# Chunked attention and a token mixer on one core: a table of steps in place of a planner, with other homes and another order for loads and stores

## The chip, the core and the metric

The kernel runs on one core of one Trainium2 chip. The core has TensorE (PE in the profile, with PEld for its weight loads), VectorE (DVE), ScalarE (ACT), GpSimd (POOL), SyncE (SP) and 16 DMA engines, with SBUF as working memory and PSUM, in eight banks, for what TensorE writes. The metric is the device time of one execution in microseconds (us): the median of three runs before the change is 141.73, with 141.18 and 142.25 as the ends. The profile is of one further execution, of 140.38 us, whose span from first to last instruction is 138.6.

## The reference

Inputs q, k and v have 8 batches, 8 heads, 576 tokens and 64 channels, all 32-bit floats. Attention is inside chunks of 64 tokens; its output, heads side by side (512 channels), goes through a mixer over tokens.

```python
scores = scale * np.matmul(q_c, k_c.transpose(0, 1, 2, 4, 3))   # chunks of 64 tokens
scores = scores - np.max(scores, axis=-1, keepdims=True)
attn = np.exp(scores)
attn = attn / (np.sum(attn, axis=-1, keepdims=True) + 1e-09)
out = np.matmul(attn, v_c)
...
x = out.transpose(0, 2, 1, 3).reshape(B, S, H * D)
wq = x @ w_q
wk = x @ w_k
W_tok = scale * np.einsum('bsd,btd->bst', wq, wk)
mixed = np.einsum('bst,btd->bsd', W_tok, x)
return (np.maximum(mixed, 0.0) @ w_out).astype(np.float32)
```

The kernel multiplies in another order: mixed = wq (wk^T x), with wk^T x a matrix of 64 by 512 for a batch, called G.

## The kernel before, in words

**Units.** Work is cut into 20 "pairs". A whole pair is 256 tokens of a batch (2 x 128); a batch has two of them and 64 tokens left over, and the left-over tokens of two batches make a small pair. For each two batches the order is whole, whole, small, whole, whole: pairs 0 to 4 are batches 0 and 1, with pair 2 small, and so on up to pair 19. Pairs 2, 7, 12 and 17 are small.

**Steps of a pair.** PE transposes q and k (`tq`, L476, L461 for a small pair), ACT or DVE copy the results to SBUF (`qbd`, `kt`), PE makes scores (`S`, L496), DVE takes the maximum and subtracts it (L509, L520), ACT takes the exponential (L530), PE transposes that (`E`, L542), it is copied (`et`), PE multiplies with v (`V`, L572, two halves of a whole pair; a column of ones beside v gives the sum), DVE divides (L584, L588, L598, tile `xs`). Then come the transposes of xs (`xT`, L614), the projection (`pj`, L624, copied to `wt`), and the transposed weights (`wkT`, L641). Per batch PE makes G (L680, copied to `g`); per pair it then makes the mixed tokens (`mix`, L721), ACT or DVE take the positive part (`rm`, L739 and L741), PE multiplies with w_out (`out`, L755) and ACT or DVE copy the result to the tile `osb`, from which SP stores it (L769 to L775). All copies are at L401.

**Shapes of the array.** Most matmuls use the whole 128 x 128 array. L476 and L680 write 64 columns ("tall" in the code), L572 works in quarters of 64 x 64 ("quart").

**Order.** A planner, `plan` (L51), runs while the program is built. It has costs and due times for each step (`RANK`, `ENGINE`), plays the engines through and emits each step on the engine and PSUM bank that it picked; on every engine the steps then stand in that fixed order. Where PE would be idle in the first 26 us of that plan it puts matmuls on a tile of ones (`idle`, L788).

**Loads.** GpSimd issues them, pair by pair: q and k, then v of the same pair; the mixer's weights come behind pair 1 (`wqk`) and pair 3 (`wo`). They convert to 16 bits on the way. Pair 0's q and k come through SP in 32 bits, into two homes of `osb`. q and k of whole pairs have 11 homes in turn (`NQK`), v of all pairs has one place each in `v_all`, `osb` has four homes (`NOSB`). Eight counters serve GpSimd's loads in turn, so a load is issued when the one eight before it has landed.

**Stores.** SP issues them in program order: the first half of a whole pair (128 tokens, 256 KB) as soon as it is copied, the second half as two stores of 128 KB since its two blocks of 64 tokens lie swapped in the tile; for a small pair two of 128 KB.

Of the kernel before, what the change touches and what calls it, by code (L numbers as in the profile page):

```python
# [17 lines left out]
class Node:  # L18


    def __init__(self, kind, prio, cost, emit, deps, forms=(), takes=(), reads=None, size=0):
        self.kind, self.prio, self.cost, self.emit = kind, prio, cost, emit
        self.deps, self.forms, self.takes, self.reads = deps, forms, list(takes), reads
        self.size = 2 * size
        self.frees = None
        self.form = self.eng = self.done = None
        if reads is not None:
            reads.readers += 1


class Banks:


    def __init__(self, n):
        self.n, self.readers, self.left, self.at, self.end = n, 0, 0, None, 0.0
        self.by = None


TAIL = {"PE": 0.17, "DVE": 0.09, "ACT": 0.1}
BEGIN = {"PE": 1.5, "DVE": 4.9, "ACT": 3.4}  # L40
SWITCH = {
    ("full", "tall"): 0.1,
    ("tall", "full"): 0.21,
    ("full", "quart"): 0.155,
    ("quart", "full"): 0.15,
    ("quart", "tall"): 0.11,
    ("tall", "quart"): 0.17,
}


def plan(nodes, look, idle, sem=0.05, banks=8):  # L51

    free_at = [0.0] * banks
    held = [False] * banks
    users, waiting = {}, {}
    for n in nodes:  # L60
        waiting[n] = sum(d.done is None for d in n.deps)
        for d in n.deps:
            users.setdefault(d, []).append(n)
    clock = dict(BEGIN)
    ready = [n for n in nodes if n.cost and not waiting[n]]
    loads = [n for n in nodes if n.kind == "load"]
    form, order = None, []
    count, fetched = 0, [0.0, 0.0, 3.0]

    def place(n, at):  # L70
        taken, spots = set(), []
        for bk in n.takes:
            best = None
            for i in range(0, banks, bk.n):
                span = range(i, i + bk.n)
                if any(held[x] or x in taken for x in span):
                    continue
                t = max(free_at[x] for x in span) + sem
                buddy = i ^ 1
                lone = bk.n == 1 and not held[buddy] and free_at[buddy] + sem <= at  # L80
                key = (max(t, at), lone, -t, i)
                if best is None or key < best[0]:
                    best = (key, i)
            if best is None:
                return None, None
            taken.update(range(best[1], best[1] + bk.n))
            spots.append(best[1])
            at = max(at, best[0][0])
        return at, spots

    while ready:
        options = {}
        for n in ready:
            there = max([d.done + sem for d in n.deps], default=0.0)
            pick = None
            for e, cost in n.cost.items():
                at = max(clock[e], there)
                if n.reads is not None and n.reads.by not in (None, e):
                    at = max(at, n.reads.end + 0.03)
                if e == "PE":  # L100
                    if form is not None and form not in n.forms:
                        at = max(at, clock[e] + SWITCH[form, n.forms[0]])
                    at = max(at, fetched[(count + n.size) // 256] - cost / 2)
                    cost *= 2 if at < COLD else 1
                if pick is None or at + cost < pick[0]:
                    pick = (at + cost, at, e)
            _, at, e = pick
            at, spots = place(n, at)
            if at is not None:
                options.setdefault(e, []).append((at, n.prio, len(order), n, spots))  # L110
        best = None
        for e, found in options.items():
            soonest = min(o[0] for o in found)
            stay = [e == "PE" and form in o[3].forms for o in found]
            some = [
                (o[1] - BONUS * same, o[0], o)
                for o, same in zip(found, stay)
                if o[0] <= soonest + (max(look, STAY) if same else look)
            ]
            o = min(some, key=lambda s: s[:2])[2]  # L120
            if best is None or o[0] < best[0]:
                best = (o[0], e, o[3], o[4])
        at, e, n, spots = best
        while e == "PE" and clock[e] < WARM:
            cols = 512 if at - clock[e] > 0.4 and clock[e] > COLD else 256
            cost = cols / (1200 if clock[e] < COLD else 2360)
            spot = next((i for i in reversed(range(banks)) if not held[i] and free_at[i] + sem < clock[e]), None)
            if spot is None or at - clock[e] <= 0.15:
                break
            emit = lambda f, spot=spot, cols=cols: idle(spot, cols)  # L130
            w = Node("idle", 0.0, {"PE": cost}, emit, [], forms=("full",), size=1)
            w.eng, w.form, form, w.start = e, "full", "full", clock[e]
            clock[e] += cost
            w.done = free_at[spot] = clock[e] + TAIL[e]
            if (count + w.size) // 256 > count // 256:
                fetched.append(w.start + FETCH[0])
            count += w.size
            order.append(w)
        for bk, i in zip(n.takes, spots):
            bk.at, bk.left = i, bk.readers  # L140
            for x in range(i, i + bk.n):
                held[x] = True
        if e == "PE":
            if form not in n.forms:
                form = n.forms[0]
            n.form = form
            if (count + n.size) // 256 > count // 256:
                fetched.append(at + n.cost[e] / 2 + (FETCH[0] if at < FETCH[2] else FETCH[1]))
            count += n.size
        n.eng, n.start = e, at  # L150
        clock[e] = at + n.cost[e] * (2 if e == "PE" and at < COLD else 1)
        n.done = clock[e] + TAIL[e]
        if n.reads is not None:
            bk = n.reads
            bk.left -= 1
            bk.end, bk.by = max(bk.end, n.done), e
            if not bk.left:
                for x in range(bk.at, bk.at + bk.n):
                    held[x], free_at[x] = False, bk.end
        if n.kind == "osb":  # L160
            for x in loads:
                if x.done > n.done:
                    x.done += STORE
        if n.frees is not None:

            late = max(n.done + HOME - x.done for x in loads if x.first == n.frees)
            for x in loads:
                if x.first >= n.frees and late > 0:
                    x.done += late
        ready.remove(n)  # L170
        for u in users.get(n, ()):
            waiting[u] -= 1
            if not waiting[u]:
                ready.append(u)
        order.append(n)
    return order


LAG = {"tq": -0.31, "S": -3.7, "E": 1.53, "V": -7.38, "x": -6.59, "xT": 2.38, "pj": -2.9, "G": -8.16, "mix": 3.34, "out": 4.56}
LOOK = 0.107  # L180
CLEAR, STAY, BONUS = 0.0, 0.0, 0.0
COLD, WARM = 5.0, 26.0
NQB, NG, NQK, NOSB = 3, 3, 11, 4
STORE, HOME = 0.7, 5.5
FETCH = (6.4, 3.7, 100.0)


RANK = [
# [62 lines left out]
def kernel(  # L251
# [31 lines left out]
    for b in range(0, B, 2):  # L283
        for bb, ms in ((b, range(NPB)), (b, [None]), (b + 1, range(NPB))):
            for m in ms:
                pairs.append((bb, m))
                first.append(NU)
                NU += 1 if m is None else 2
# [99 lines left out]
    def vec(n):  # L388
        return n / 960 + 0.066
# [434 lines left out]
```

## Time and profile before

| | |
|---|---|
| median of three runs | 141.73 us |
| profiled execution | 140.38 us |
| its span | 138.6 us |
| PE, DVE, ACT, POOL busy | 127.3, 114.0, 98.5, 74.0 us |
| matmuls on ones (L788) | 73, 16.2 us busy |
| loads (software queue) | 14.29 MB written to SBUF in 78736 packets |
| store and first-load queue | 10.49 MB in 7584 packets |
| HBM read, written | 29.62 MB, 9.44 MB |

The profile's slices cut the span into 40 parts and give the busy tenths of each engine in each part. A line of the timeline has the start, the time it took, the engine, the line of the code, the operation, and in brackets how long the engine was idle before it and what ended that. PE's matmuls overlap each other in such rows, so the step between starts tells more than the time taken. A load's or a store's landing is when its completion is counted.

### The profile page before, as it was taken

To read this page: it belongs to the slowest core of one execution; us is meant where nothing else is said; L and a number is where in the kernel's file an instruction comes from. 1 tells how busy PE (TensorE), PEld (TensorE's weight loads), DVE (VectorE), ACT (ScalarE), POOL (GpSimd) and SP (SyncE) were. 2 spreads that over 40 slices of the span, in tenths; PEclk is the share of its full clock that TensorE was granted. 3 is DMA by queue.
4 is the path that set the end of the run, shared out by engine and by line. 5 is a ranking of instruction groups with operands and counts; after the bars stand their busy time and mean duration, and the time that the engine had idled before them with its cause. 6 is when DMAs were issued, how large, how long until landed. Compare 5 with 4: busy or idle time off the path is not lost.

```text
span 138.6 us, 5196 instructions
## 1 busy us (share of the span) xinstructions
PE 127.3 (92%) x2205; PEld 89.5 (65%) x2205; DVE 114.0 (82%) x223; ACT 98.5 (71%) x177; POOL 74.0 (53%) x95
## 2 busy tenths in 40 slices
PE   6999999989997999989999999899997999899950
PEld 4566577667676676777767786687676666665410
DVE  4777969579999999999999999989989798871510
ACT  3255584668883998878968968977596497895730
POOL 7997998576499677344898555629900000000000
PEclk9999999999999999999999999999999999999998
DMA  3999999999999999999999999999999943315484
GB/s 92 271 176 155 140 162 179 172 178 169 165 263 203 202 173 215 238 224 200 155 204 220 238 173 206 212 200 188 190 225 264 127 137 90 123 34 137 168 236 142
DMA packets 86343, 25.11 MB, mean 181 GB/s; under 512 B 79152, under 2 KB 81712, under 8 KB 86320
## 3 DMA queue, kind: packets, MB, share of 16 engines
q0 software_dynamic: 78736, 14.29, 127.4%
q1 hardware_dynamic: 7584, 10.49, 24.4%
q8 instruction: 17, 0.28, 0.7%
q14 instruction: 6, 0.05, 0.1%
HBM read 29.62 MB, written 9.44 MB: 282 GB/s over the span
## 4 chain that ended last, share of the span: by engine, by line
PE 59%; DVE 26%; ACT 8%; issue 4%; DVEq 0%
PE ps L755 15%; PE ps L476 10%; PE ps L788 6%; PE ps L721 5%; DVE mx L509 5%; PE ps L496 5%; PE ps L614 4%; DVE xs L598 4%; PE ps L542 4%; DVE sh L520 4%; PE ps L624 4%; PE ps L572 3%; ACT es L530 2%; DVE xt L401 2%; DVE qbd L401 2%
## 5 line engine op out<-in xcount | busy, mean ns | idle before, releaser
L755 PE MATMUL ps<-wo,rm 128*128 128x512 f16 x144 | 36.0, 379 | 0.0
L356 POOL DMA_DIRECT2D v_all<-in_v_dram x32 | 28.9, 919 | 2.5 <-DMA wo<-in_moe_w_out_dram 1.5
L509 DVE TENSOR_REDUCE mx<-ps 128x16 f32<-128x1024 f32 (+1 forms) x20 | 22.3, 1114 | 4.4 <-PE ps L496 2.0
L598 DVE TENSOR_TENSOR xs<-ps,rec 128x512 f16<-128x512 f32 x36 | 24.0, 687 | 0.4
L401 ACT COPY osb<-ps 128x512 f32<-128x512 f32 x30 | 17.5, 587 | 5.9 <-PE ps L755 5.6
L530 ACT ACTIVATE es<-sh 128x1024 f16<-128x1024 f32 (+1 forms) x20 | 19.5, 974 | 2.3 <-DVE sh L520 1.8
L476 PE MATMUL ps<-ident,qk 128*64 128x128 f16 x512 | 20.6, 222 | 0.3
L476 PEld LDWEIGHTS <-qk 128*64 128x64 f16 x512 | 16.0, 109 | 6.7 <-issue 4.3
L520 DVE TENSOR_TENSOR sh<-ps,mx 128x1024 f32<-128x1024 f32 x16 | 19.5, 1219 | 0.3
L755 PEld LDWEIGHTS <-rm 128*128 128x128 f16 x144 | 12.5, 98 | 11.0 <-ACT rm L741 0.4
L401 ACT COPY qbd<-ps 64x512 f32<-64x512 f32 (+1 forms) x29 | 15.5, 536 | 4.1 <-PE ps L476 3.6
L741 ACT ACTIVATE rm<-ps 128x1024 f16<-128x1024 f32 (+1 forms) x14 | 16.1, 1164 | 2.4 <-PE ps L721 2.2
L788 PE MATMUL ps<-ones 128*128 128x256 f16 (+1 forms) x73 | 16.2, 346 | 1.5 <-DVE ones L300 1.2
L344 POOL DMA_DIRECT2D qk<-in_k_dram x15 | 13.5, 902 | 4.8 <-DMA qk<-in_k_dram 4.2
L344 POOL DMA_DIRECT2D qk<-in_q_dram x15 | 13.6, 906 | 4.5 <-DMA qk<-in_q_dram 2.6
L496 PEld LDWEIGHTS <-qbd 128*128 128x128 f16 x288 | 10.6, 98 | 3.5 <-issue 1.3
L496 PE MATMUL ps<-kt,qbd 128*128 128x64 f16 x288 | 11.7, 193 | 0.7 <-DVE xs L598 0.4
L542 PE MATMUL ps<-ident,es 128*128 128x128 f16 x144 | 11.3, 220 | 0.5 <-ACT es L530 0.4
L614 PE MATMUL ps<-ident,xs 128*128 128x128 f16 x144 | 11.2, 219 | 0.2 <-DVE xs L598 0.2
L721 PE MATMUL ps<-wt,g 128*128 128x256 f16 (+1 forms) x96 | 10.8, 246 | 0.5 <-DVE g L401 0.3
L624 PE MATMUL ps<-xt,wqk 128*128 128x256 f16 (+1 forms) x80 | 10.9, 262 | 0.0
L572 PE MATMUL ps<-v_all,et 64*64 64x65 f16 x576 | 9.6, 195 | 1.4 <-issue 1.1
(56 smaller groups left out, 181.7 us busy)
## 6 DMA issues: line engine op xcount, KB each, us to landing
out_dram<-osb SPq DMA_DIRECT2D x40, 128.0 KB, 5.2
v_all<-in_v_dram POOLq DMA_DIRECT2D x32, 128.0 KB, 9.0
out_dram<-osb SPq DMA_DIRECT2D x16, 256.0 KB, 5.7
qk<-in_q_dram POOLq DMA_DIRECT2D x15, 256.0 KB, 8.8
qk<-in_k_dram POOLq DMA_DIRECT2D x15, 256.0 KB, 9.4
osb<-in_q_dram SPq DMA_DIRECT2D x1, 512.0 KB, 4.0
osb<-in_k_dram SPq DMA_DIRECT2D x1, 512.0 KB, 5.0
qk<-in_q_dram POOLq DMA_DIRECT2D x8, 64.0 KB, 8.3
```

Source lines behind the costliest of these rows:

```text
L344: nc.gpsimd.dma_start(qk[u][:, t], rows)
L356: nc.gpsimd.dma_start(v_all[:, first[u] + i, :, 0:D], rows)
L401: (nc.vector.tensor_copy if eng == "DVE" else nc.scalar.copy)(to, of)
L476: nc.tensor.transpose(tp[half(o), j, :, r, :], of, ident[:])
L496: nc.tensor.matmul(sp[:, i, j, c, :], lhsT=st["qb", u][:, j, x].rearrange("p o s -> p (o s)"), rhs=st["kt", u][:, j, x * C : x * C + C], s ...
L509: nc.vector.tensor_reduce(mx[:], scores(), axis=AX.X, op=ALU.max)
L520: nc.vector.tensor_tensor(out=sh[:].rearrange("p x (g r) -> p x r g", r=R), in0=in_banks(bs, 512).rearrange("p i (x r g) -> p (i x) r g", ...
L530: nc.scalar.activation(es[:].rearrange("p x s -> p (x s)"), st["sh", u][:].rearrange("p x s -> p (x s)"), AF.Exp, scale=scale_attn,)
L598: nc.vector.tensor_tensor(out=to, in0=xp()[:, :, :, 0:D], in1=by, op=ALU.mult)
L721: nc.tensor.matmul(ma[:, o, f, s], lhsT=st["g", bb][:, c0 : c0 + P], rhs=st["wt", u][:, s], start=True, stop=True,)
L755: nc.tensor.matmul(op[c, :], lhsT=st["rm", u][:, f, i * P + c.start : i * P + c.stop], rhs=wo[:, f, :], start=(f == 0), stop=(f == NF - 1),)
L788: nc.tensor.matmul(ps[:, i, 0:cols], lhsT=ones[:, 0:P], rhs=ones[:, 0:cols], start=True, stop=True)
```

## The change

The planner and its tables go; the program has one table, `ORDER`, with a step, its engine (p, a, v) and its PSUM bank in each word, and `i` for a matmul on ones with its bank and its columns. The table has 63 of those where the planner put 73. `HOMES` gives each tile its number of homes: q and k of whole pairs 7, `osb` 13, `wt` and `wk` 8 where they had 6. v of whole pairs goes into a ring of 8 homes of two slots each (`NV`); small pairs keep their own. `LOADS` gives the order of loads: q and k of the next pair stand ahead of v of this one. A load of v into a used home is emitted right behind the product with v of the pair that had it (`load_more`).

Before the first store SP gets a small read of `v_all`, into a tile `held`. A whole pair is stored in two stores of 256 KB (64 partitions, two blocks each) once both halves are copied. The second half of the last pair is made and stored in two parts of 256 columns, and its v is loaded turned, in two loads, so that its tokens lie in order.

```diff
+NQB, NG, NV = 3, 3, 8
...
+HOMES = {
+    "qk": 7,
+    "osb": 13,
...
+LOADS = "q1 v0 q2 v1 wqk v2 q3 v3 wo q4 q5 v4 q6 v5 q7 v6 q8 v7 q9 v8 q10 v9 q11 v10 q12 v11 q13 v12 q14 v13 q15 v14 q16 v15 q17 v16 q18 v17 q19 v18 v19"
+ORDER = """
+1a 0v 3v 2a i7.256 i6.256 i5.256 i7.256 i6.256 i5.256 i7.256 i6.256 i5.256 i7.256 i6.256 i5.256 i7.256 i6.256
...
+448a 309a 503a 524p1 449p0 422p7 397p6 525v 483v 423a 450v 504p4 424p7 558p0 555p5 526v 484v 398v 505a 425a
...
+615v 551p5 608p2 609v 623a 624p4 616p6 620p7 552a 625a 610p4 618p5 612p2 617v 621v 613v 611a 619a
+"""
-    v_all = const.tile([P, NU, H, VW], F16, name="v_all")
+    v_all = const.tile([P, 2 * NV + B // 2, H, VW], F16, name="v_all")
...
+    heir_v = dict(zip(whole, whole[NV:]))
+    slot = {u: 2 * (n % NV) for n, u in enumerate(whole)}
+    slot.update({u: 2 * NV + n for n, u in enumerate(rests)})
...
+    made_v = {None: 2}
+
+    def load_more():
+        while loads and made_v.get(loads[0][2], 0) == 2:
+            load, args, _ = loads.pop(0)
+            load(*args)
+
+    load_more()
...
+            def pe_v(fours=fours, xp=xp):
...
+                made_v[u] = made_v.get(u, 0) + 1
+                load_more()
...
+            wide = DM // 2 if (b, m, i) == (B - 1, NPB - 1, 1) else DM
+            for at in range(0, DM, wide):
...
+                def ev_o(eng, i=i, bo=bo, s=s, wide=wide):
+                    if not osb:
+                        osb.append(home("osb", [P, 2, DM], F32))
+                    copy(eng, osb[0][:, i, s], in_banks(bo, wide)[:, 0])
+                    if not held:
+
+                        held.append(const.tile([1, 2], F16, name="held"))
+                        last = slot[len(pairs) - 1]
+                        nc.sync.dma_start(held[0][:], v_all[P - 1 : P, last + 1, H - 1, D - 2 : D])
+                    done.append(s)
+                    if m is None:
+                        for c in range(2):
+                            nc.sync.dma_start(out[b + c, S - C : S, :], osb[0][half(c), i, :])
+                    elif turned(u, 1):
+                        t0 = 2 * P * m + i * P
+                        nc.sync.dma_start(out[b, t0 : t0 + P, s], osb[0][:, i, s])
+                    elif len(done) == 2:
+                        rows = out[b, 2 * P * m : 2 * P * m + 2 * P, :].rearrange("(x p) d -> p x d", p=C)
+                        for c in range(2):
+                            nc.sync.dma_start(rows[:, 1:3] if c else rows[:, 0:4:3], osb[0][half(c)])
...
+    steps = [n for n in nodes if n.cost]
+    for e in ORDER.split():
+        what, eng, *at = re.split(r"([ipav])", e, maxsplit=1)
+        at = [int(x) for part in at for x in part.split(".") if x]
+        if eng == "i":
+            nc.tensor.matmul(ps[:, at[0], 0 : at[1]], lhsT=ones[:, 0:P], rhs=ones[:, 0 : at[1]], start=True, stop=True)
+            continue
+        n = steps[int(what)]
+        for bk, i in zip(n.takes, at):
+            bk.at = i
+        n.emit(*{"p": (), "a": ("ACT",), "v": ("DVE",)}[eng])
```

More of the change, by code (lines that the diff above doesn't have):

```diff
@@ L1 @@
 import math
+import re
 from contextlib import ExitStack
@@ L18, with __init__ @@
 class Node:
[L21 to L26, printed above, removed]
+    def __init__(self, kind, cost, emit, deps, form=None, takes=(), reads=None, size=0):
+        self.kind, self.cost, self.emit, self.deps = kind, cost, emit, deps
+        self.form, self.takes, self.reads, self.size = form, list(takes), reads, 2 * size
+        self.frees = self.pair = self.done = None
         if reads is not None:
@@ L34, in __init__ @@
     def __init__(self, n):
[L35 to L47, printed above, removed]
-}
[L51 to L176, printed above, removed]
@@ L273 @@
     VW = D + 2
-    QUART, TALL, FULL = ("quart",), ("tall",), ("full",)
+    QUART, TALL, FULL = "quart", "tall", "full"
     const = ctx.enter_context(tc.tile_pool(name="const", bufs=1))
-    work = ctx.enter_context(tc.tile_pool(name="work", bufs=3))
+    work = ctx.enter_context(tc.tile_pool(name="work", bufs=1))
     psum = ctx.enter_context(tc.tile_pool(name="psum", bufs=1, space=PS))
     ctx.enter_context(tc.manual_schedule())
-    pairs, first, NU = [], [], 0
+    pairs = []
     for b in range(0, B, 2):
@@ L312, in half, with turned, home @@
         return slice(C * i, C * i + C)
+    def turned(u, i):
+        return u == len(pairs) - 1 and i == 1
+    def home(tag, shape, dtype=F16):
+        return work.tile(shape, dtype, name=tag, tag=tag, bufs=HOMES[tag])
     arrive, clk, wide_in = {}, 4.6, []
+    whole = [u for u, (b, m) in enumerate(pairs) if m is not None]
+    heir = dict(zip(whole[1:], whole[1 + HOMES["qk"] :]))
+    heir_v = dict(zip(whole, whole[NV:]))
+    rests = [u for u, (b, m) in enumerate(pairs) if m is None]
+    slot = {u: 2 * (n % NV) for n, u in enumerate(whole)}
+    slot.update({u: 2 * NV + n for n, u in enumerate(rests)})
     def landing(key, us):
@@ L357, in load_v @@
-        landing(("v", u), halves if m is None else 2 * halves)
-    whole = [u for u, (b, m) in enumerate(pairs) if m is not None and u]
-    heir = dict(zip(whole, whole[NQK:]))
-    for u in range(len(pairs)):
-        load_qk(u)
-        if u == 0:
-            make_identity(nc, ident[:])
-        load_v(u)
-        if u == 1:
-            for i, x in enumerate((moe_w_q, moe_w_k)):
-                nc.gpsimd.dma_start(wqk[:, :, i, :], x.rearrange("(f p) j -> p f j", p=P))
+        if m is None:
+            for i in range(2):
+                rows = v[b + i, :, S - C : S, :].rearrange("h p d -> p h d")
+                nc.gpsimd.dma_start(v_all[half(i), slot[u], :, 0:D], rows)
+            return
@@ new lines, in load_v, with load_w @@
+        for i in range(2):
+            t0 = 2 * P * m + i * P
+            for c in range(2) if turned(u, i) else [None]:
+                on, of = (slice(0, P), slice(t0, t0 + P)) if c is None else (half(1 - c), slice(t0 + c * C, t0 + c * C + C))
+                nc.gpsimd.dma_start(v_all[on, slot[u] + i, :, 0:D], v[b, :, of, :].rearrange("h p d -> p h d"))
+    def load_w():
+        for i, x in enumerate((moe_w_q, moe_w_k)):
+            nc.gpsimd.dma_start(wqk[:, :, i, :], x.rearrange("(f p) j -> p f j", p=P))
@@ L369, with load_wo @@
+    def load_wo():
+        nc.gpsimd.dma_start(wo[:], moe_w_out.rearrange("(f p) n -> p f n", p=P))
+    load_qk(0)
+    make_identity(nc, ident[:])
+    arrive["f32", 0], arrive["f32", 1] = 4.85, 6.2
+    loads = []
+    for e in LOADS.split():
+        u = int(e[1:]) if e[1:].isdigit() else None
+        rest = u is not None and pairs[u][1] is None
+        if e == "wqk":
             landing("w", 0.9)
-        if u == 3:
-            nc.gpsimd.dma_start(wo[:], moe_w_out.rearrange("(f p) n -> p f n", p=P))
+            loads.append((load_w, [], None))
+        elif e == "wo":
@@ L372 @@
             landing("wo", 3.3)
+            loads.append((load_wo, [], None))
+        elif e[0] == "q":
+            for t in range(2):
+                landing(("qk", u, t), 0.94 if rest else wide)
+            loads.append((load_qk, [u], None))
+        else:
+            landing(("v", u), halves if rest else 2 * halves)
+            loads.append((load_v, [u], next((w for w in heir_v if heir_v[w] == u), None)))
+    made_v = {None: 2}
[3 more added lines that the diff above has]
+            load(*args)
@@ L415 @@
             cost = {"ACT": act(512, True), "DVE": 0.4}
-            ready.setdefault(("cast", t), []).append(add("cast", -9.0, cost, ev, [landed(("f32", t))]))
+            ready.setdefault(("cast", t), []).append(add("cast", cost, ev, [landed(("f32", t))]))
     parts = [(("qb", n + 2), t[:], 0.95) for n, t in enumerate(qbd[2:])]
@@ L461, in pe @@
                         nc.tensor.transpose(tp[:, t, j, :], qk[u][:, t, 2 * j : 2 * j + 2, :], ident[:])
-            n1 = add("tq", pri, {"PE": 8 * 0.056}, pe, [landed(("qk", u, 1))], forms=FULL, takes=[bk], size=8)
+            n1 = add("tq", {"PE": 8 * 0.056}, pe, [landed(("qk", u, 1))], form=FULL, takes=[bk], size=8)
             for t in range(2):
@@ L476, in pe @@
                             nc.tensor.transpose(tp[half(o), j, :, r, :], of, ident[:])
-            n1 = add("tq", pri, {"PE": 8 * 0.056}, pe, ready["cast", t] if u == 0 else [landed(("qk", u, t))], forms=TALL, takes=[bk], size=16)
+            n1 = add("tq", {"PE": 8 * 0.056}, pe, ready["cast", t] if u == 0 else [landed(("qk", u, t))], form=TALL, takes=[bk], size=16)
             if u in heir:
```

263 lines of the change are left out of this document (127 added, 136 removed), and 39 rows, old and new, of the table RANK.

## The prediction

> **What bounds the kernel now.** I read the page first (shares, slices), then the stretches, the timeline of TensorE, and the landing of each load against its first use.
>
> In the page's slices PE, DVE and the DMA are all near full, at different ends:
>
> ```profile
> PE   6999999989997999989999999899997999899950
> ...
> DVE  4777969579999999999999999989989798871510
> ...
> DMA  3999999999999999999999999999999943315484
> GB/s 92 271 176 155 140 162 179 172 178 169 165 263 203 202 173 215 238 224 200 155 204 220 238 173 206 212 200 188 190 225 264 127 137 90 123 34 137 168 236 142
> ...
> L788 PE MATMUL ps<-ones 128*128 128x256 f16 (+1 forms) x73 | 16.2, 346 | 1.5 <-DVE ones L300 1.2 <-DVE ones L304 0.3
> ```
>
> Until 26.6 us PE is kept busy with L788, matmuls on ones that fill the wait for loads. After that there are none, and the DMA stays full until 110 us. Two stretches (columns: PE, PEld, DVE, ACT, POOL, granted clock, DMA share, GB/s):
>
> ```profile
> 32.60:133.60 101.00, 96.99 (x1711) 68.68 (x1709) 89.70 (x173) 80.29 (x145) 46.60 (x57) 1.00 1.50 186
> ...
> 30.00:100.00 70.00, 67.51 (x1280) 49.63 (x1277) 67.76 (x128) 56.70 (x101) 48.13 (x60) 1.00 1.88 201
> ```
>
> PE and DVE are both at 96 to 97% from 30 to 100 us, so a gain needs relief on both. The PE timeline shows where busy PE is not working:
>
> ```profile
> 64.25 1.03 PE L755 MATMUL ps<-wo,rm 128*128 128x512 f16 x4
> 65.21 0.64 PE L476 MATMUL ps<-ident,qk 128*64 128x128 f16 x16
> 65.77 0.32 PE L572 MATMUL ps<-v_all,et 64*64 64x65 f16 x16
> 66.03 0.81 PE L476 MATMUL ps<-ident,qk 128*64 128x128 f16 x16
> ```
>
> Four L755 take 0.865 when another such group follows, but 0.96 here, where the array's shape changes from 128x128 to 128x64. I added up, from starts in such rows, what each step takes back to back (transposes of q or k 0.57, scores 0.47, transposed weights 0.45, half of the product with v 0.19, xT 0.45, projection 0.44, G 0.55, mix 0.44, out 0.865; less for the small pairs). All steps come to 105.0 us. When the transposes of k of pair 5 start (32.61, 0.04 after that load landed) 90.5 are left; PE ends at 133.57, so 100.96 us hold 90.5 of work. The other 10.4 hold 67 changes of shape: **0.155 each**, small waits included.
>
> Loads against first use: q and k of pairs 1 to 5 land 0.0 to 0.8 us before PE takes them, later pairs' 1 to 5.7 us, v of every pair 6 to 15 us. Thus q and k are late, v is early. Undisturbed, q or k takes 1.44 us of the stream and half of v 0.84. The whole stream ends at 110.4 and would end near 91 without the 5.6 MB of stores served before it: 3.4 us per MB (windows of it give 2.7 to 3.5).
>
> After PE:
>
> ```profile
> 133.60 0.59 ACT L401 COPY osb<-ps 128x512 f32<-128x512 f32 x1 [0.23 <-PE ps L755]
> 133.84 0.54 SPq L771 DMA_DIRECT2D out_dram<-osb  x1
> 134.47 1.11 SPq L775 DMA_DIRECT2D out_dram<-osb  x2
> ```
>
> The last of these lands at 137.35, the span ends at 138.6: 5.05 us after PE. The profiled execution took 140.38, 1.78 more than its span, and 1% less than the median of 141.73.
>
> **The change, part by part.** Up to pair 4 nothing arrives sooner in the end: q4 stands behind the same set of loads in both. q1 comes two halves of v (1.7) sooner and q2, q3 likewise in part, which is covered by fewer L788 (63 for 73). q5 stands ahead of v4, so its k lands at 32.57 - 1.7 = 30.9. From the start of q4's transposes (26.57) to those of k5 the new order has 3.9 us of work, the old 4.7; with its five changes of shape PE gets there at about 31.4, with 0.45 more left to do: **-0.75** net.
>
> The new table has 49 changes of shape from there on against 67: 18 x 0.155 = **-2.8** (by the barest change, 0.095, -1.7). This counts only if DVE lets it: between the scores of pair 4 and the last xs it was busy 87.4 of 92.3 us. The table gives DVE seven full-size q/k copies fewer (0.68 each), four xt fewer (0.69), three g more (0.42), one clear and one osb more, a few smaller ones fewer: some 5 us off DVE there. ACT, busy 74.4 of those 92.3, gets about 4 more: room remains. PE then would end at 130.0.
>
> **The gate.** The store queue gets a read of the last slot of v ahead of all stores. But in the ring that slot has two tenants, pairs 9 and 19. The read is emitted with the first output copy, pair 19's load only after the product with v of pair 9, later in the table. In the built instruction list the read waits for the 47th load, the second half of v9, and pair 19's load waits for the read. So stores are held to the landing of v9, near 52.8 (now 53.5, less 3.6 for the 1.05 MB stored before it, plus 2.9 for q10 put ahead), not to the last load. Behind the waiting read only stores queue on SP, and 13 homes hold the three pairs ready by then: no engine waits. Stores, two of 256 KB a pair after both halves, then mix with loads as now.
>
> Is a load late? Take its landing now, less the v that moves behind it, less 3.4 per MB that is stored later; against its need, counted back from 130.0 with the work and changes left. q12: 68.4 - 1.7 - 0.9 = 65.8; needed 66.2. q17, which the table takes right behind pair 16: 96.2 - 1.7 - 2.5 (3.67 MB stored for 4.4) = 92.0; needed at 130.0 - 36.35 - 15 x 0.155 = 91.3. That is late by 0.7. The bounds are 0 (2.7 us per MB) and 2.5 (pair 8's 0.5 MB also ahead); I take **+0.7**, since q17's own surroundings, 87.5 to 97, give 3.0 per MB. v of all pairs keeps over 4 us, so the ring costs nothing; q, k homes (7 for 11) come free 30 us early.
>
> **The tail.** Last on PE is the second half of pair 18. DVE copies it (0.69, not 0.59 on ACT); then SP issues that pair's two stores and only then the last quarter of pair 19, ready long before: the last issue is the third behind the copy, not the second. From PE's end: 0.03 + 0.69 + 0.28 + 0.52 + 0.68 = 2.2, and 2.4 to land, against 3.8 now: **+0.8**. Bounds: 0, if the last one lands inside the pair's stores, and 1.2.
>
> Sum: -0.75 - 2.8 + 0.7 + 0.8 = -2.05. Span 136.55, execution 138.33, a ratio of 0.985: **139.7 us** as a median. A measurement of this kernel tells about 1% from no change.
>
> **Rivals.** (1) *Loads never bind*, because stores really stay behind the last load (the change doing what it says) or stores cost 2.7: the 0.7 goes, and DVE's relief of 5 may take another 1 us out of the waits: 138.0, down to 136.8. Against the first: the wait in the list. (2) *Given back*: changes of shape worth only 0.095 (-1.7) and q17 late by its bound (2.5) give -0.75 - 1.7 + 2.5 + 0.8 = +0.85, 142.6; halfway from the forecast to that, -0.6, 141.1. For it: that q4 sets the pace at first, whatever the fillers. (3) *Slower: the flush.* When v9 lands, three pairs (1.57 MB, 5.3 us of DMA) are let go at once beside q11 and q12, with 1 to 3 us and 0.4 us in hand. The trace has one such place: q19's two loads took 3.16 and 2.64 instead of 1.44 each while 1 MB of stores landed. If PE loses over 3.5 us there it is slower; with 5.3 all on q12 and q17 late after it, +2: 143.8.
>
> The trace has the loads at about half pace in that place. [...]
>
> **How the numbers follow.** Forecast 0.44 (three quarters of it over 1% faster), rival 1 0.22, rival 2 0.16 (within 1%), rival 3 0.18. So faster 0.55, same 0.27, slower 0.18. The range leaves out half of rival 3's far end and the tip of rival 1: 136.8 to 143.0.
>
> **What would show it.** The first store issued near 52 us with two or three pairs close behind, and loads still running after 100; if no store is issued before 85, rival 1's reading of the gate holds. L788 at 63, tall stretches fewer, DVE under 95% between 30 and 100. PE idle or waiting on q, k of pairs 12 and 17 by at most 1 us each; over 3 us together is rival 3. From PE's end to the span's 5.8 us. I am wrong outright if ACT, with 4 us more in the middle, is what PE waits for, or if PE reaches k5 later than 31.5.

## Result and profile after

Over 20 runs each the changed kernel has a median of 140.45 us (138.57 to 141.75), the kernel before 141.54 (140.9 to 145.68). The ratio is **0.9883**, with an interval of 0.9852 to 0.9913: 1.2% or some 1.7 us faster. All ratios here leave out executions more than 1.5% above the fastest of their kernel (7 of the 20 of the change, half of those of e3, e5 and e9); by medians of all executions the change stands at 0.992, e3 at 0.988, e5 at 0.989 and e9 at 1.005. The forecast was 139.7 us, a ratio of 0.985.

The profiled execution took 141.11 us, with a span of 139.3 and a mean granted clock of 0.973. Eleven of the 20 executions had a mean clock of 0.971 to 0.978 and a median of 140.72 us, the other nine one of 0.982 to 0.993 and 139.47. So stretches are compared below rather than spans.

The slices and the group of matmuls on ones, from the page of the kernel after:

```profile
PE   6979969989999989999989999949999999999900
...
DVE  5459989679899999989997999937789998887410
...
PEclk9999999999999999999999999995999999999995
DMA  3999999999999999999999999999999705074884
GB/s 93 263 163 155 100 172 183 182 175 174 157 162 175 169 177 177 159 278 211 288 223 213 231 249 174 191 155 243 185 162 273 226 4 152 4 168 124 255 239 123
...
L691 PE MATMUL ps<-ones 128*128 128x256 f16 (+1 forms) x63 | 14.4, 360 | 1.2 <-DVE ones L154 1.2
```

PE and DVE are still near full in the middle. New is a hole in both near slice 27 (93 us), with half the clock in the slice after it. The two stretches (columns: PE, PEld, DVE, ACT, POOL, granted clock, DMA share, GB/s), from the taking of pair 5's k to PE's end and from 30 to 100 us:

```profile
32.17:132.58 100.41, 96.23 (x1723) 71.13 (x1718) 87.31 (x167) 81.93 (x154) 48.99 (x60) 0.98 1.54 185
30.00:100.00 70.00, 65.91 (x1275) 50.87 (x1275) 62.62 (x118) 59.92 (x111) 48.48 (x60) 0.98 1.90 199
```

DVE is busy 89% of the second stretch, where it was 97%; ACT has more than before. SP's rows show when the stores begin:

```profile
55.27 0.75 SPq L663 DMA_DIRECT2D held<-v_all  x1
56.08 2.32 SPq L674 DMA_DIRECT2D out_dram<-osb  x3
```

The second half of pair 9's v lands at 55.26, and the small read goes 0.01 later. The last load lands at 107.53: stores and loads mix for 50 us. PE where the shape changes (L365 is the transposes of q and k, L462 the product with v, L647 the product with w_out), and then around pair 17 (L350):

```profile
62.70 1.03 PE L647 MATMUL ps<-wo,rm 128*128 128x512 f16 x4
63.65 1.08 PE L365 MATMUL ps<-ident,qk 128*64 128x128 f16 x32
64.67 0.45 PE L462 MATMUL ps<-v_all,et 64*64 64x65 f16 x32
65.05 1.04 PE L647 MATMUL ps<-wo,rm 128*128 128x512 f16 x4
...
92.52 0.38 PE L350 MATMUL ps<-ident,qk 128*128 128x128 f16 x4 [0.78 <-DMA qk<-in_q_dram]
93.68 0.38 PE L350 MATMUL ps<-ident,qk 128*128 128x128 f16 x4 [0.78 <-DMA qk<-in_k_dram]
93.90 1.46 PE L647 MATMUL ps<-wo,rm 128*128 128x512 f16 x4
95.15 1.06 PE L508 MATMUL ps<-ident,xs 128*128 128x128 f16 x8
```

Work of one shape now stands in longer stretches: q and k of a pair together, both halves of the product with v together. At pair 17 PE waits twice for a load, 1.56 us in all, and what follows is slow: L647 takes 1.46 for what takes 1.03, L508 1.06 for 0.61, until 97.7 us. The end:

```profile
132.62 0.69 DVE L291 COPY osb<-ps 128x512 f32<-128x512 f32 x1 [1.58 <-PE ps L647]
133.38 1.30 SPq L674 DMA_DIRECT2D out_dram<-osb  x2
134.77 0.62 SPq L670 DMA_DIRECT2D out_dram<-osb  x1
```

PE ends at 132.58, the last store lands at 138.20, the span ends at 139.34: 6.76 us after PE, where it was 5.05.

### The profile page after: what moved, and what is told of

It is laid out like the page before. It is cut to its first block, busy times and chain, and to the rows that moved or that the text cites. A ratio compares the mean times of both kernels' runs of the same rounds, so it can differ in the third digit from the quotient of the medians.

```text
span 139.3 us, 5152 instructions
## 1 busy us (share of the span) xinstructions
PE 124.1 (89%) x2199; PEld 91.0 (65%) x2199; DVE 112.2 (81%) x217; ACT 99.5 (71%) x184; POOL 74.5 (53%) x96
## 4 chain that ended last, share of the span: by engine, by line
PE 47%; DMA 27%; DVE 10%; ACT 5%; issue 4%; POOL 2%; POOLq 0%; DVEq 0%
PE ps L647 14%; DMA qk<-in_k_dram 14%; DMA v_all<-in_v_dram 8%; DMA qk<-in_q_dram 5%; PE ps L365 5%; PE ps L508 5%; PE ps L385 4%; PE ps L518 4%; PE ps L612 4%; PE ps L462 3%; DVE mx L398 3%; PE ps L572 2%; PE ps L431 2%; DVE sh L409 2%; PE ps L691 2%
## 5 line engine op out<-in xcount | busy, mean ns | idle before, releaser
L647 PE MATMUL ps<-wo,rm 128*128 128x512 f16 (+1 forms) x148 | 36.4, 377 | 0.1
L365 PE MATMUL ps<-ident,qk 128*64 128x128 f16 x512 | 18.7, 221 | 3.4 <-DMA qk<-in_q_dram 1.2
L291 ACT COPY qbd<-ps 64x512 f32<-64x512 f32 (+1 forms) x32 | 18.0, 562 | 3.5 <-PE ps L365 3.2
L365 PEld LDWEIGHTS <-qk 128*64 128x64 f16 x512 | 15.8, 110 | 6.9 <-DMA qk<-in_k_dram 2.0
L647 PEld LDWEIGHTS <-rm 128*128 128x128 f16 x148 | 13.4, 98 | 10.3 <-issue 0.2
L291 ACT COPY osb<-ps 128x512 f32<-128x512 f32 (+1 forms) x26 | 15.0, 586 | 4.4 <-PE ps L647 4.3
L632 ACT ACTIVATE rm<-ps 128x1024 f16<-128x1024 f32 (+1 forms) x12 | 13.5, 1140 | 4.4 <-PE ps L612 4.4
L691 PE MATMUL ps<-ones 128*128 128x256 f16 (+1 forms) x63 | 14.4, 360 | 1.2 <-DVE ones L154 1.2
L508 PE MATMUL ps<-ident,xs 128*128 128x128 f16 x144 | 11.8, 224 | 0.6 <-issue 0.5
L291 ACT COPY et<-ps 128x512 f32<-128x512 f32 (+1 forms) x17 | 9.4, 551 | 2.6 <-PE ps L431 1.1
L508 PEld LDWEIGHTS <-xs 128*128 128x128 f16 x144 | 9.5, 101 | 2.3 <-issue 1.3
```

Of the source, the lines that this page charges most:

```text
L291: (nc.vector.tensor_copy if eng == "DVE" else nc.scalar.copy)(to, of)
L365: nc.tensor.transpose(tp[half(o), j, :, r, :], of, ident[:])
L508: nc.tensor.transpose(tx[:, f, i, :], xs[u][:, i, 2 * f : 2 * f + 2, :], ident[:])
L647: nc.tensor.matmul(in_banks(bo, wide)[:, 0], lhsT=st["rm", u][:, f, i * P : i * P + P], rhs=wo[:, f, s], start=(f == 0), stop=(f == NF - 1),)
L691: nc.tensor.matmul(ps[:, at[0], 0 : at[1]], lhsT=ones[:, 0:P], rhs=ones[:, 0 : at[1]], start=True, stop=True)
```

## Experiments

Each kernel was run beside the kernel before; ratios are to that.

| run | edit | ratio | interval |
|---|---|---|---|
| the change | | 0.9883 | 0.9852 to 0.9913 |
| e1 | stores behind the last load | 0.9701 | 0.9646 to 0.9756 |
| e2 | pair 17's transposes later | 0.9903 | 0.9857 to 0.9950 |
| e3 | other order of the last copies | 0.9749 | 0.9685 to 0.9813 |
| e4 | e1 and 24 more changes of shape | 0.9781 | 0.9742 to 0.9821 |
| e5 | no read ahead of the stores | 0.9801 | 0.9734 to 0.9868 |
| e6 | loads in the order of before | 0.9989 | 0.9947 to 1.0031 |
| e7 | e1, copies back to DVE | 1.0625 | 1.0547 to 1.0703 |
| e8 | pair 17's wait filled | 0.9886 | 0.9829 to 0.9942 |
| e9 | kernel before with a lighter DVE | 0.9952 | 0.9910 to 0.9995 |
| e10 | e1 again | 0.9764 | 0.9712 to 0.9816 |
| e11 | e1 and e3 | 0.9690 | 0.9633 to 0.9747 |
| e12 | e11, one last store on ACT's queue | 0.9661 | 0.9607 to 0.9715 |

### The gate on the stores

**e1 and e10.** The small read is emitted behind pair 19's load, and every store behind it on SP.

```diff
+        if not loads and not held:
+            held.append(const.tile([1, 2], F16, name="held"))
+            ...
+            for to, of in waiting:
+                nc.sync.dma_start(to, of)
...
+    def store(to, of):
+        if held:
+            nc.sync.dma_start(to, of)
+        else:
+            waiting.append((to, of))
```

> The changed kernel with the store gate moved: the read of v is emitted behind the load of pair 19, and all stores are put on SP's queue behind it, so that they really wait for the last load. My theory (stores let go at the landing of v9 make q17 late, and the wait also drops PE's clock): q17 lands about 8 us before its use, the waits of 0.78 + 0.78 us and the stretch at 0.83 of the clock from 90 to 100 us go, loads end near 95 us instead of 107.5, and the time falls by 1.6 to 3.5 us, to a ratio of 0.965 to 0.977 against the kernel before. Rival (the wait at q17 is cover for other waits, DVE's or ACT's): PE waits there for something else and the ratio stays at 0.985 to 0.99. Second rival (the backlog of some 4.7 MB let go near 95 us keeps later outputs waiting for a home or delays the last stores): slower than the changed kernel, over 0.99.

> The kernel with all stores behind the last load once more, beside the next two: ratio 0.965 to 0.976, as in its first run (0.970).

0.9701 is in the middle of what was expected and 0.9764 just past its upper end: 1.2 to 1.8% (1.7 to 2.6 us) below the changed kernel. From the timeline and the stretches of e10 (L365 is pair 17's transposes here):

```profile
90.83 0.62 PE L365 MATMUL ps<-ident,qk 128*128 128x128 f16 x8
...
95.15 0.75 SPq L265 DMA_DIRECT2D held<-v_all  x1
...
31.77:128.62 96.85, 94.51 (x1724) 70.24 (x1719) 87.19 (x167) 81.65 (x154) 48.92 (x60) 1.00 1.60 188
```

Pair 17's eight transposes run in one row without a wait, 7.9 us after their last load has landed. The loads end at 95 and not at 107.5, and from the taking of pair 5's k to its end PE needs 96.85 us. So the stores that mix with loads do cost time in the changed kernel, and 13 homes for outputs are enough to hold all of them back.

**e5.** The read is left out and each store goes when its copies are done.

> The changed kernel without the small read ahead of the stores: SP issues each store as soon as its copies are done, the first near 38 us instead of 56. My reading (3.4 us of load stream per MB stored): about 1.5 MB goes out between 38 and 55, so q8 to q12 land up to 5 us later than in the changed kernel, and PE, with 1 to 3 us in hand at pairs 8 and 9 and 0.5 at pairs 13 and 14, is stopped there as well; at q17 the total stored is about the same as before, so the wait there stays near 1.6. Time 0 to 1.5 us above the changed kernel, ratio to the kernel before 0.988 to 1.000. Rival: the read does nothing since it waits for the wrong load; then ratio 0.984 to 0.992 and q17 late by the same 1 us. If instead the wait at q17 goes away, the read itself and the three pairs let go at once are what made q17 late, and the ratio falls to 0.965 to 0.980.

The first store went at 42.3 us and not at 56.1. The ratio, from three executions, is 0.8% below that of the change, and the two intervals just overlap: the read, where it stands, brings nothing that can be told, and may cost up to 1%. Its profile can't say why. In it pair 17's last load lands 2.1 us earlier than in the change, of which 1.2 is an earlier first load, and PE comes later as well, since it stood still for 2 us with no engine or load named as the cause (such stops are looked at in the last section):

```profile
52.15 0.49 PE L509 MATMUL ps<-ident,xs 128*128 128x128 f16 x6 [1.96 <-issue]
52.57 0.44 PE L463 MATMUL ps<-v_all,et 64*64 64x65 f16 x16
52.95 1.89 PE L648 MATMUL ps<-wo,rm 128*128 128x512 f16 x4
```

Whether pair 17 would be late without that stop stays open.

**e2.** Pair 17's transposes and their three copies move behind the scores of pair 16.

```diff
-... 439v 520p6 523v 440v 393p7 394v 522v 521v 420p1 ...
+... 439v 440v 393p7 394v 420p1 395p4 396a 500p2 501v 502v 520p6 523v 522v 521v 421a ...
```

> The changed kernel with one edit: the transposes of pair 17 and the three copies behind them stand after the scores of pair 16, about 2.2 us of PE work later, and the stores stay as they are. If the wait for q17 and the clock that drops behind it are what costs, PE finds q17 landed, the clock stays at 1.00 from 90 to 100 us and 1.5 to 3.5 us go: a ratio of 0.965 to 0.978. If the moved copies only make the wait reappear at the scores of pair 17 or at the copies, it is 0.985 or more.

The loads are then in time (taken at 95.18, landed at 92.93), and nothing is gained, 0.9903. The wait has moved:

```profile
95.18 0.61 PE L351 MATMUL ps<-ident,qk 128*128 128x128 f16 x8
...
99.12 3.17 PE L648 MATMUL ps<-wo,rm 128*128 128x512 f16 x8 [2.44 <-DVE qbd L292]
```

L648 needs the bank that pair 17's transposes hold until DVE has copied them, and DVE now gets to that later. Here one step can't be moved by itself, since each bank of the table already has its next user.

**e8.** Eight matmuls on ones of 512 columns stand ahead of pair 17's transposes, on the bank that these write.

```diff
-520p6
+i6.512 i6.512 i6.512 i6.512 i6.512 i6.512 i6.512 i6.512 520p6
```

> The changed kernel with eight matmuls on ones of 512 columns ahead of the transposes of pair 17, where PE stood still 0.78 + 0.78 us for q and k and then showed matmuls at twice their time until 97.7 us. They take about 8 x 0.216 = 1.7 us, as long as the wait. If the standstill is what makes PE slow afterwards, PE's granted clock stays at 1.00 between 90 and 100 us and the time falls by the 1.9 us that the slow stretch cost, less what the filling overruns: ratio 0.974 to 0.981. If the slow stretch has another cause, it stays and the ratio is that of the changed kernel or above: 0.986 to 0.996.

```profile
90.96 1.90 PE L691 MATMUL ps<-ones 128*128 128x512 f16 x8
92.70 0.61 PE L350 MATMUL ps<-ident,qk 128*128 128x128 f16 x8
93.14 1.03 PE L647 MATMUL ps<-wo,rm 128*128 128x512 f16 x4
```

In the profile the filling does what was expected of it: PE is ready at 90.96, is kept busy to 92.70, and the L647 behind it takes 1.03 and not 1.46; the granted clock is 1.00 between 90 and 100 us. In this execution too pair 17 is late: one of its two loads of k lands at 91.83. By the ratio it brings nothing: 0.9886 against 0.9883, where 0.974 to 0.981 was expected. Filling a wait doesn't shorten it, and what the slow stretch costs can't be told from these two ratios. The list of executions speaks for a price: those of the change with a mean clock of 0.971 to 0.978 take 1.25 us more in the median than the nine others, and five of the six of e8 are of the second kind (0.984 to 0.995). That the low clock is this stretch in each of them isn't shown, for only one is traced.

### Where PE's gain came from

**e4.** In the kernel of e1, a matmul of four columns in the full shape goes between the halves of twelve products with v: 24 more changes of shape.

```diff
+        if e in BETWEEN:
+            nc.tensor.matmul(ps[:, at[0], 500:504], lhsT=ones[:, 0:P], rhs=ones[:, 0:4], start=True, stop=True)
```

> The first of these kernels (stores behind the last load) with a matmul on ones of four columns in the full shape put between the two halves of the product with v in 12 pairs from pair 4 on: 24 changes of the array's shape and 12 small matmuls more, nothing else. If PE bounds those stretches and a change costs 0.155 us, it is slower than the first kernel by 24 x 0.155 = 3.7 plus about 0.4 for the matmuls, 4.1 us; by the barest change of 0.095, 2.7 us. If DVE bounds them, as its 96 to 97% in the kernel before would allow, it is slower by less than 1 us.

```profile
66.71 0.32 PE L477 MATMUL ps<-v_all,et 64*64 64x65 f16 x16
66.97 0.18 PE L708 MATMUL ps<-ones 128*128 128x4 f16 x1
67.08 0.32 PE L477 MATMUL ps<-v_all,et 64*64 64x65 f16 x16
67.33 1.04 PE L662 MATMUL ps<-wo,rm 128*128 128x512 f16 x4
```

In place the two halves take 0.62 us (66.71 to 67.33) where they took 0.38 in e10: 0.12 for each change, the small matmul included. But the ratio is only 0.8% above e1's, of the same set of runs: 1.1 us, or 0.05 for each. The traces give a little more, 1.9 us from pair 6's transposes to PE's end (92.57 in e1, 94.48 here), 0.08 each; 0.5 of the 1.9 is one longer stop, 0.89 at 53.4 us where e1 has 0.39. By these figures about half of each change or more falls into time that PE would have waited anyway. At 0.155 it should have been 3.7 us.

**e9.** The kernel before, with a maximum that leaves out half of the keys in nine pairs, in the same order of steps. The trace has these at 0.69 us instead of 1.22, so 4.8 us less on DVE.

```diff
+            half_of = scores()[:, :, 0:32] if u in (5, 6, 8, 9, 10, 11, 13, 14, 15) else scores()
-            nc.vector.tensor_reduce(mx[:], scores(), axis=AX.X, op=ALU.max)
+            nc.vector.tensor_reduce(mx[:], half_of, axis=AX.X, op=ALU.max)
```

> The kernel before, with the same order, shapes, loads and stores, and DVE made lighter: the maximum of nine whole pairs (5, 6, 8 to 11, 13 to 15) is taken over half of the keys, so that each takes about 0.66 us and not 1.22. That is 9 x 0.56 = 5.0 us off DVE in the middle, what the prediction said the table takes off it. It leaves out the other half of the keys in that maximum. Theory now (a change of shape is worth 0.06 us, the rest of the lost time in the kernel before was PE held by DVE): PE comes 2.5 to 3.5 us sooner, ratio 0.975 to 0.983. The prediction's reading (changes of shape carry the 10.4 us, DVE only allows a gain): under 1 us, ratio 0.993 to 1.000.

0.9952: 0.7 us of the 4.8 arrive by the ratio, and none by the medians. My theory after e4, that PE had been held by DVE's load, falls; here the prediction's reading (DVE only allows) is the better one.

**e7.** In the kernel of e1, eleven copies go from ACT to DVE and three the other way, each at its place in the table.

```diff
-... 191a ... 251a ... 276a ... 405a ... 430a ... 474a ... 499a ... 182a ... 207a ... 292a ... 421a ...
+... 191v ... 251v ... 276v ... 405v ... 430v ... 474v ... 499v ... 182v ... 207v ... 292v ... 421v ...
-... 298v ... 387v ... 452v ...
+... 298a ... 387a ... 452a ...
```

> The kernel with all stores behind the last load (ratio 0.970, no wait for a load after 45 us), with copies of its middle put back where the kernel before had them by number: seven full-size q or k copies and four xt from ACT to DVE (pairs 5 to 16), three of G from DVE to ACT. That is 7 x 0.68 + 4 x 0.69 - 3 x 0.42 = 6.3 us more on DVE, whose idle time between 33 and 100 us is some 5.5 us. Shape changes and loads stay as they are. Theory now: most of what PE gained came from DVE, and the changes of shape are worth only 0.06 us each; then PE waits for DVE again by 2 to 4 us and the ratio rises to 0.984 to 1.000. Rival, the prediction's: the shapes carry the gain and DVE only allows it; DVE is then full again at 97%, as it was before, and costs at most 1 us: ratio 0.970 to 0.978.

1.0625, 13 us above e1: far outside both expectations. The two stretches from 40 us on, PE's waits and one row:

```profile
40.00:50.00 10.00, 9.75 (x162) 7.70 (x162) 7.62 (x15) 6.21 (x14) 10.00 (x13) 0.83 1.97 173
50.00:60.00 10.00, 7.48 (x139) 5.91 (x139) 7.52 (x18) 3.70 (x7) 7.08 (x9) 0.83 2.16 167
...
PE ps L662 <- DVE kt L306: 3.5, 2, 1.9
PE ps L533 <- DVE xt L306: 3.2, 2, 2.4
...
40.23 1.86 PE L662 MATMUL ps<-wo,rm 128*128 128x512 f16 x4 [1.93 <-DVE kt L306]
```

DVE isn't full here (7.6 and 7.5 of 10, though 9.3 to 9.6 in the stretches from 30 and from 60 to 80 us); each engine stands waiting for the other. Pair 6's k is an example: on ACT (e1) its copy starts at 38.68, 0.3 us after its transposes end; on DVE here it starts at 39.49, behind a subtraction and a division, 2.7 us after they end, and L662 in the row above waits for it. So in this table PE feels the place of each copy in the order more than the amount of DVE's work. It is no measure of "DVE relief", since the order wasn't made again for it.

The waits view says the same of the change itself: PE's waits on other engines from pair 5's k on, in the kernel before and then (last row) in e10. Its columns are the time in all, the number and the longest.

```profile
PE ps L680 <- ACT wk L401: 0.5, 2, 0.4
PE ps L461 <- DVE xs L598: 0.4, 1, 0.4
PE ps L496 <- ACT kt L401: 0.3, 1, 0.3
PE ps L721 <- DVE g L401: 0.3, 1, 0.3
PE ps L542 <- ACT es L530: 0.3, 1, 0.3
...
```

```profile
PE ps L477 <- DVE sh L424: 0.2, 1, 0.2
```

With three more of 0.2 that the kernel before has, 2.4 us of such waits became 0.2, on ACT and DVE alike.

### Loads and tail

**e6.** The changed kernel with the old order of loads.

```diff
-LOADS = "q1 v0 q2 v1 wqk v2 q3 v3 wo q4 q5 v4 q6 v5 ..."
+LOADS = "v0 q1 v1 wqk q2 v2 q3 v3 wo q4 v4 q5 v5 q6 v6 ..."
```

> The changed kernel with the loads in the order of the kernel before (v of a pair ahead of q and k of the next). The prediction's step: q5.k lands 1.3 to 1.7 us later, so PE reaches it 0.5 to 1.3 later; q12, q13, q14 and q16, which land 0.5 to 3 us ahead of their use in the changed kernel, become late by up to 1.2, and q17's wait grows from 1.6 to about 3. Sum +2 to +4 us, ratio to the kernel before 1.002 to 1.017. Rival: the loads' order is covered by other slack (v was 6 to 15 us early, but PE is held by q4 at first in both orders, and later only at q17): under +1, ratio 0.984 to 0.995.

0.9989: 1.1% or 1.5 us above the change, so the order of loads is worth that much, between the two expectations. PE takes pair 5's k at 34.01, 1.84 later than in the change, although the first load of all landed 1.28 earlier in this execution (7.64 against 8.92; it is half of v here and not q, some 0.6 shorter). PE is behind as early as pair 4, whose transposes start at 29.24 and not at 27.40.

**e3.** The last quarter of pair 19 is copied and stored ahead of the second half of pair 18.

```diff
-617v 621v 613v 611a 619a
+617v 621v 611a 619a 613v
```

> The changed kernel with the last five copies emitted in another order, so that the last quarter of pair 19 is stored ahead of pair 18's two stores and not behind them; PE, ACT and DVE keep their order. By the step of the tail in the prediction (the last issue is the third behind the last copy) the time from PE's end to the span's end falls from 6.7 us by 0.6 to 1.0: a ratio of 0.981 to 0.984. If instead the landing of the two stores of 256 KB sets the end, it falls by under 0.3 and the ratio stays at 0.987 to 0.99.

```profile
132.06 1.69 SPq L671 DMA_DIRECT2D out_dram<-osb  x3
133.16 0.69 DVE L292 COPY osb<-ps 128x512 f32<-128x512 f32 x1 [1.58 <-PE ps L648]
133.88 1.30 SPq L675 DMA_DIRECT2D out_dram<-osb  x2
```

Two issues and not three stand behind the last copy, and the span ends 6.02 us after PE: 0.74 less, in the trace. The ratio, 0.9749, is lower than that explains, from four executions and with a wide interval; I take the size from the trace.

**e11 and e12.** The same in the kernel of e1, and then with one of pair 18's two stores issued by ACT.

```diff
+                            put = nc.scalar.dma_start if (b, m, c) == (B - 1, 0, 1) else store
-                            store(rows[:, 1:3] if c else rows[:, 0:4:3], osb[0][half(c)])
+                            put(rows[:, 1:3] if c else rows[:, 0:4:3], osb[0][half(c)])
```

> All stores behind the last load, and the last quarter of pair 19 copied and stored ahead of the second half of pair 18, so that two issues and not three stand behind the last copy on SP. The prediction's tail step: the third issue cost 0.68 and the landing starts that much later, so 0.6 to 0.8 us below the kernel without this, ratio 0.962 to 0.968. Rival: the end is set by the bytes of the stores still queued, which are the same: within 0.2 us of it.

> As the run before it, with the second of pair 18's two stores issued by ACT, idle by then, beside SP's first one. If issues one behind the other on SP set the end, another 0.6 us less: ratio 0.958 to 0.964. Rival: both stores share the DMA engines, so the last lands when it did; ratio 0.962 to 0.968.

0.9690 and 0.9661. From PE's end to the span's it is 7.7 us in e10, 7.3 in e11 and 5.8 in e12. The steps have the expected sign, but both ratios lie just above the range expected, that of e12 inside its rival's, the intervals of neighbours overlap, and even those of e12 and e10 (1.0% or 1.5 us apart) just touch. The 1.5 us from e11 to e12 in the traces speak for the issues one behind the other on SP. e12 beats both kernels: 136.78 us as a median where the kernel before had 141.63.

## Why the prediction was right, and where it was not

**Total.** A ratio of 0.985 was forecast and 0.9883 measured, inside the range. But all four terms of the sum were off, and they cancelled: PE's gain was larger than forecast, the start gave less, the wait at pair 17 and the tail cost more. That the total came out near is in part luck.

**Start, -0.75: right in kind.** PE took pair 5's k at 32.17, not at 31.4; -0.44 and not -1.2 against the 32.61 of before, which with the 0.45 more left to do makes nothing. (26.57 + 3.9 + 5 x 0.155 is 31.25 and not 31.4.) The prediction had named a k5 later than 31.5 as a sign of being wrong outright, and in ten of the eleven profiles with this order of loads it is later, up to 33.65 in e4. In e5 pair 4's transposes start as they did before, at 26.58, and k5 follows at 31.34: the work up to it was right. What wasn't seen is that the first load's landing moves from one execution to the next: it was 8.92 in this profile and 8.16 and 8.26 in e10 and e11, which took k5 at 31.77. By e6 the order of loads is worth 1.5 us over the whole kernel.

**Changes of shape, -2.8: the step that failed.** Neither size nor reason held. Free of the wait at pair 17, e10 needs 96.85 us where the kernel before needed 100.96, 4.1 less for 0.45 more work: the gain on PE was 4.5 and not 2.8. The 10.4 us beyond work had been divided by 67 changes, "small waits included". Set against the median step between starts within a row of the same kind, the 67 changes of before are 51 that cost 0.11 each and 16 that cost 0.2 to 0.6, waits among them; the 49 of e10 are 40 with 0.12 and nine with 0.2 to 0.33. All together they fall from 11.6 to 7.4 us, 3.4 of it in the long ones. e4 prices a change at 0.05 to 0.08, so 18 fewer are worth 0.9 to 1.4. Waits on ACT and DVE that the view names went from 2.4 us to 0.2. About 1 us of the 4.5 is named by neither. DVE's lighter load by itself is not the cause (e9). What is left, by e7 and the waits view, is the order of the table on ACT and DVE: each result there when PE comes for it. This part is argued and not shown: e7 tells what misplaced copies cost in the new table, not that the planner's stood wrong, and a run of the old order with the new one's copies wasn't made.

**Gate: right, and shown.** The read waits for the second half of v9, as read out of the order of emission; it went at 55.27, not at 52.8, and three pairs of outputs followed within 8 us. e1 is what the change doesn't do.

**q17, +0.7: right place, too small.** Pair 17's last load landed at 93.55, forecast 92.0, and PE waited 1.56 us, inside the bounds of 0 to 2.5. By e1 and e10 the mixing of stores with loads costs 1.7 to 2.6 in time. q12 came at 63.1, 3.3 ahead of its use.

**Tail, +0.8: outside its bounds.** It was +1.7. The third issue went 2.19 us after PE's end, as worked out (2.2), but took 3.43 to land and not 2.4: it stands behind two stores of 256 KB issued just before. The landing had been taken from a place where less was queued.

**Rivals.** The first one's time (138.0, down to 136.8) is what e1 and e10 gave, 137.2 and 138.2: it was right about the worth of a real gate, and wrong that the change has one. The flush of the third didn't stop PE: behind the ten stores that went from 56 to 66 us, q and k of pair 13 landed 2.15 and 4.01 us apart from the load before, 6.2 for what takes 2.9, and k still came 0.5 us ahead of PE. The loads kept about half of their pace, as at q19's place in the trace of before.

**DVE and ACT.** DVE fell to 89% between 30 and 100 us (93% in e10, which has no hole there), below the 95% named; ACT rose to 60 of 70 us and held PE nowhere by more than 0.3 us.

## To carry to other kernels

A wait counts for what has been emitted when it is emitted: a read meant as a gate on the last load, of a place with two tenants, waits for the first of them (here at 55.27 us, 0.01 behind the second half of v9; emitted behind the last load, as in e10, at 95.15), and SP's timeline shows at once at which load it opens. Don't price a kind of event by dividing all lost time by its number: split the events into those that cost the same each time and those where something was waited for, and test the price by adding some. Where three engines stand in a fixed order, the place of a copy can matter more than the load of its engine: here 13 us (e7) against 0.7 (e9).

## What was not expected of the hardware

- **Half speed after a standstill of PE.** After 0.78 + 0.78 us within 2 us (the change), 1.22 (e1, at 20 us), 1.93 (e7), 1.96 (e5) and 2.44 (e2) the next matmuls took up to twice their time, L648 1.89 for four where it takes 1.03. After a single 1.1 (the kernel before, the product with v) and 0.7 us (e10) they did not, nor with the wait filled (e8). The length alone doesn't decide: e9 stood still for 1.94 us and went on at full speed.

```profile
108.75 0.19 PE L573 MATMUL ps<-v_all,et 64*64 64x65 f16 x1 [1.94 <-issue]
...
109.32 1.03 PE L756 MATMUL ps<-wo,rm 128*128 128x512 f16 x4
```

In the change's trace the granted clock is 0.50 for 3.41 us, from 94.36 to 97.77, and 1.00 for the 88.75 us ahead of that, 26 times as long. In the 3.41 us just before (90.95 to 94.36) PE is busy for 1.42 and stands still for 1.99. With the 88.75 us cut into steps of this length, no other step has more than 1.04; in the kernel before, at 1.00 up to PE's end, none has more than 1.08. Windows of 10 us show 0.83 once in e1, e2, e3 and e5 and twice in e7, as much as 3.41 us at half speed makes. What length of standstill brings it was not shown.
- **Stops at the same places of the program.** PE stands for 0.3 to 2.0 us in twelve of the fourteen profiles ("issue"), and waits there for no engine and no load that the profile names. The places are fixed: near the 859th, 1369th or 1624th matmul with the new table (in e8 also near the 1751st), near the 1884th in the kernel before and in e9. In the change two such stops, 0.46 and 0.47 us long, both end 1.48 us after the end of a transfer of 16 KB on the DMA queue that the page calls "instruction" (51.48 and 91.38, behind 50.00 and 89.90); in the kernel before the one of 1.08 us ends 1.22 us after one (107.75, behind 106.53). Most of the 17 such transfers in each of these traces come without a stop. Whether PE waits for what they bring was not shown, and no run tests it.
- **The first load's landing** came between 7.71 (e5) and 9.04 us (e4) in eleven profiles with the same order of loads, and what follows moves with it until PE becomes the bound.
